# Attention weights turned by 32x32 blocks on the vector engine and 16 DMAs a group, in place of PE transposes

## The chip, the cores and the metric

The kernel runs on one core of a Trainium2 chip. The metric is the device time of one launch in microseconds (us). A core has five engines that run side by side, each through its own instructions in their order: PE (matrix products; its weight loads are shown as PEld), DVE (vectors), ACT (activations and copies), POOL (not used here beyond the first microsecond) and SP, whose queue only issues DMAs. A DMA can also be issued from ACT's queue. Engines wait for one another, and for DMAs to land, on semaphores.

## The reference

A chunked attention feeds a channel mix. All inputs are float32.

```python
# attention: 8 batches, 8 heads, 576 positions, head size 64; chunks of 64 positions
scores = scale * (q_c @ k_c.T)                    # 64 x 64 in each chunk
attn = exp(scores - max) / (sum + 1e-9)
x = (attn @ v_c)  ->  (batch, position, 512)
# channel mix
x_prev = x shifted by one position inside its batch
xk = mu_k * x + (1 - mu_k) * x_prev
xr = mu_r * x + (1 - mu_r) * x_prev
k = relu(xk @ w_k)                                # 512 -> 1024
out = sigmoid(xr @ w_r) * ((k * k) @ w_v)         # 512 -> 512, 1024 -> 512
```

## The kernel before

The 4608 positions are worked through in 18 groups of 256, each of two tiles of 128 positions (two chunks each). The matrix products of the channel mix run in three passes, since each operand is split into a high and a low part (`hi`, `lo`): `pk` is `xk @ w_k`, `pr` is `xr @ w_r`, `pv` is `k*k @ w_v`.

Steps are recorded by `do(fn, engine)` under a task's name and played back in an order written out by hand: `START` for the opening (groups 0 and 1, and the loading and splitting of weights), and then `GROUP`, once for each of the groups 2 to 17. Nothing reorders them afterwards; an engine's queue is what `GROUP` says. In `GROUP`, a word is a task, with a dot and the numbers of its steps (all, where there are none). For group g:

- `K0` to `K3` are four quarters of the k-branch of group g itself: product on PE, then relu, square, `hi` on ACT and `lo` on DVE. `R0`, `R1`: product and sigmoid. `V0`, `V1`: steps 0 to 7 are eighths of the product, step 8 multiplies by the sigmoid on DVE (L672) and issues the DMA of `out` from SP. The letter's digit is the tile.
- `Sa`, `Sb` are the scores and the softmax of the next group's tiles a and b (2g+2, 2g+3): step 0 product `s`, 1 row maximum, 2 subtraction, 3 exp on ACT, 4 sums, 5 division. `Pa`, `Pb` are their values: step 0 turns the weights on PE into `pt`, 1 copies them to `pT` on ACT, 2 is the product `xps` with `v`, 3 and 4 bring it to `x` in SBUF (the copy of L131 on ACT).
- `Mka`, `Mkb`, `Mra`, `Mrb` mix x with its predecessor on DVE (`d` L510, `mixk` and `mixr` L540, `lo` L559, with `hi` on ACT between), which gives `xk` and `xr` of the next group.
- `Tc`, `Td` turn q and k of the tiles 2g+4 and 2g+5 in 32x32 blocks on DVE (L339), which the next group's `Sa` and `Sb` read. `Lq`, `Lk`, `Lv` issue the loads of q and k for group g+3 and of v for group g+2 from SP.

Loads of q and k come as 16 DMAs each, because a DMA here moves one band of 32 partitions of one head pair. A group of 256 positions that crosses the end of a batch of 576 takes 32 DMAs each: `segments` cuts it. That is so for the groups 6, 11, 13 and 15, whose loads are issued in the groups 3, 8, 10 and 12. They are called cut groups below; in the groups 15 and 16 nothing is left to load of q and k.

Attention weights have 128 rows (positions) and 512 columns (8 heads by 64 keys). For `xps` they must have the keys on the partitions. Before, four transposes through PE with an identity matrix do this for a tile, and one copy on ACT takes them from PSUM.

PSUM pools bound how far products run ahead: `ps_k` has two buffers for `pk`, `ps_o` two for `pr` and `pv`, `ps_s` one for `s` and `pt`. `relu`, `out` and the loads' tiles have two buffers.

Of the kernel before, what the change touches and what calls it, by code (L numbers as in the profile page):

```python
# [7 lines left out]
F32 = mybir.dt.float32  # L8
# [8 lines left out]
P = 128  # L17
CH = 64
TT = 128
G = 256  # L20
# [32 lines left out]


GROUP = """
Lq K0.0 Sa.0 Sb.0 Sa.12 K0.123 Sa.3 Sb.12 K0.4 Sb.3 Sa.45 Sb.45 K1 K2.0 Pa.0 K2.1234 Pa.1
K3.0 Pb.0 Pb.1 K3.1234 Tc R0 Pa.2 Pb.2 Pa.34 Pb.34 Lv Lk Mka R1 Mkb Mra Mrb Td V0 V1
"""


# [18 lines left out]
def tile_chunk_attention_channel_mix(  # L79
# [12 lines left out]
    nc = tc.nc  # L92
    B, H, S, D = q.shape
    DM, FF = w_k.shape
    w_k, w_v, w_r = (w.bitcast(I32) for w in (w_k, w_v, w_r))
    HP = H // 2
# [2 lines left out]
    NCH = S // CH  # L99
    NG = B * S // G  # L100
    out_f = out.rearrange("b s c -> (b s) c")
    engine = dict(A=nc.scalar, D=nc.vector, G=nc.gpsimd)

    const = ctx.enter_context(tc.tile_pool(name="const", bufs=1))
    wts = ctx.enter_context(tc.tile_pool(name="wts", bufs=1))
# [1 line left out]
    tmp = ctx.enter_context(tc.tile_pool(name="tmp", bufs=2))  # L107
# [9 lines left out]
    do = Steps()  # L117
    T = {}
# [10 lines left out]
    def copy(e, to, x):  # L129
        if e == "A":  # L130
            nc.scalar.activation(to, x, AF.Copy)  # L131
        elif e == "D":
            nc.vector.tensor_copy(out=to, in_=x)  # L133
        else:
            nc.gpsimd.tensor_scalar(to, x, 1.0, 0.0, ALU.mult, ALU.add)
# [38 lines left out]
    def load_v(t):  # L174
        do.task = f"v{t}"

        def fn(_):
            vt = T[f"v{t}"] = att.tile([P, HP, 2, D], F32, tag="v", name=f"v_{t}", bufs=2)
            for e in range(2):
                b, c = divmod(2 * t + e, NCH)  # L180
                for j in range(2):
                    nc.sync.dma_start(  # L182
                        out=vt[j * CH : (j + 1) * CH, :, e, :],
                        in_=v[b, j * HP : (j + 1) * HP, c * CH : (c + 1) * CH, :].rearrange(
                            "h t d -> t h d"
                        ),
                    )

        do(fn, "Q")

    def load_blocks(g):
        for nm, src in (("q", q), ("k", k)):
            do.task = f"b{nm}{g}"

            def fn(_, nm=nm, src=src):
                dst = T[f"{nm}{g}"] = ld.tile([P, HP, G // 32, 32], F32, tag=nm, name=f"{nm}_{g}")
                for s, n in segments(g * G, G):
                    b, t0 = divmod(g * G + s, S)
                    for j in range(2):
                        for dh in range(2):  # L200
                            pp = j * 64 + dh * 32
                            for hp in range(HP):
                                nc.sync.dma_start(
                                    out=dst[pp : pp + 32, hp, s // 32 : (s + n) // 32, :],
                                    in_=src[
                                        b, j * HP + hp, t0 : t0 + n, dh * 32 : (dh + 1) * 32
                                    ].rearrange("(t i) d -> i t d", i=32),
                                )

            do(fn, "Q")  # L210
# [16 lines left out]
    def wv_tile(s, h):  # L227
        if (s, h) not in wv:
            wv[s, h] = wts.tile([P, NF // 2, DM], F32R, tag=f"wv{s}_{h}", name=f"wv{s}_{h}")
        return wv[s, h]  # L230
# [76 lines left out]
    halves = [slice(j * CH, (j + 1) * CH) for j in range(2)]  # L307
# [22 lines left out]
    def att_qk(t):  # L330

        g, tl = divmod(t, 2)
        tb = slice(tl * (TT // 32), (tl + 1) * (TT // 32))
        part = slice(tl * TT, (tl + 1) * TT)
        do.task = f"T{t}"
        for nm, to in (("q", qT), ("k", kT)):

            def f_move(_, nm=nm, to=to):
                nc.vector.transpose(  # L339
                    out=to[:, :, part].rearrange("p h (t i) -> p h t i", i=32),  # L340
                    in_=T[f"{nm}{g}"][:, :, tb, :],
                )

            do(f_move, "D")
# [59 lines left out]
    def x_cuts(t):  # L404

        cut = -t * TT % S
        if 0 < cut < TT:
            return [(0, cut, 0), (cut, TT - cut, cut + 1)]
        return [(0, TT, 0)]

    def att_values(t):
        do.task = f"P{t}"

        g, tl = divmod(t, 2)

        def f_tr(_):
            if tl == 0:
                T[f"pt{g}"] = ps_s.tile([P, 2, HP, TT], F32, tag="s", name=f"pt_{g}")
            for hp in range(HP):
                nc.tensor.transpose(  # L420
                    out=T[f"pt{g}"][:, tl, hp, :],
                    in_=T[f"p{t}"][:, 2 * hp : 2 * hp + 2, :],
                    identity=ident,
                )

        def f_pT(e):
            pT = T[f"pT{t}"] = att.tile([P, HP, TT], F32, tag="pT", name=f"pT_{t}")
            copy(e, pT, T[f"pt{g}"][:, tl])

        def f_pv(_):  # L430
            if tl == 0:
                T[f"xps{g}"] = ps_x.tile([P, NB, G], F32, tag="x", name=f"xps_{g}")
            for a in range(HP // 2):
                for e in range(2):
                    for c in range(2):
                        for j in range(2):
                            hp = 2 * a + c
                            nc.tensor.matmul(  # L438
                                T[f"xps{g}"][
                                    halves[c], 2 * j + a, tl * TT + e * CH : tl * TT + (e + 1) * CH  # L440
                                ],
                                T[f"v{t}"][halves[j], hp, e, :],
                                T[f"pT{t}"][halves[j], hp, halves[e]],
                                start=True,
                                stop=True,
                            )

        def f_open(_):

            x = xt[t] = xp.tile([P, NB, TT + 2], F32, tag="x", name=f"x_{t}")  # L450
            for s, n, c in x_cuts(t):
                if (t * TT + s) % S == 0:
                    nc.vector.memset(x[:, :, c : c + 1], 0.0)
                else:
                    seg = x_cuts(t - 1)[-1]
                    last = seg[2] + seg[1]
                    nc.vector.tensor_copy(
                        out=x[:, :, c : c + 1], in_=xt[t - 1][:, :, last : last + 1]
                    )

        def f_x(e):
            xps = T[f"xps{g}"][:, :, tl * TT : (tl + 1) * TT]
            for s, n, c in x_cuts(t):
                copy(e, xt[t][:, :, c + 1 : c + 1 + n], xps[:, :, s : s + n])

        do(f_tr, "P")
        do(f_pT, "A")
        do(f_pv, "P")
        do(f_open, "D")
        do(f_x, "A")  # L470
# [217 lines left out]
    for i in range(4):  # L688
        h = i // 2
# [5 lines left out]
            lambda s, h=h, part=part: wv_tile(s, h)[:, part, :],  # L695
            ("kk0", "kk1", "st", "st")[i],
        )
    for t in range(6):
        move_qk(t)
        att_scores(t)  # L700
        att_values(t)
        x_mix(t)
        if t in (1, 3):
            g = t // 2
            for fp in range(NF // 2):
                moe_k(g, fp)
            for tl in range(2):
                moe_r(g, tl)
# [9 lines left out]
    with tc.manual_schedule():  # L718
        for word in START.split():
            name, _, e = word.partition(":")  # L720
# [9 lines left out]
    def group(g):  # L730
        if g + 3 < NG:
            load_blocks(g + 3)
        if g + 2 < NG:
            for t in (2 * g + 4, 2 * g + 5):
                load_v(t)
                att_qk(t)
        if g + 1 < NG:
            for t in (2 * g + 2, 2 * g + 3):
                att_scores(t)
                att_values(t)  # L740
                x_mix(t)
        for fp in range(NF // 2):
            moe_k(g, fp)
        for tl in range(2):
            moe_r(g, tl)
            moe_v(g, (tl,))
        steps = do.take()
        tile_of = dict(zip("abcd", range(2 * g + 2, 2 * g + 6)))
        for word in GROUP.split():
            task, _, numbers = word.partition(".")  # L750
            if task == "Lv":
                names = [f"v{2 * g + 4}", f"v{2 * g + 5}"]
            elif task[0] == "L":
                names = [f"b{task[1]}{g + 3}"]
            elif task[-1] in tile_of:
                names = [f"{task[:-1]}{tile_of[task[-1]]}"]
            else:
                names = [f"{task[0]}{g}{task[1:]}"]
            for name in names:
                for i in numbers or range(NF + 1):  # L760
                    if f"{name}.{i}" in steps:
                        fn, e = steps.pop(f"{name}.{i}")
                        fn(e)
        assert not steps
# [30 lines left out]
```

## Time and profile before

| | |
|---|---|
| median of 3 runs | 617.06 us (616.78 to 619.68) |
| the profiled execution | 620.49 us, its span 618.7 us |
| mean granted TensorE clock | 0.988 |
| PE busy | 601.6 us (97%) |
| DVE, ACT busy | 399.8 us (65%), 332.5 us (54%) |
| chain that ended last, share of PE | 91% |
| transposes `pt` on PE | 144 instructions, 22.0 us busy |
| copies `pT` on ACT | 36 instructions, 21.3 us busy |

Times within the span are counted from the first instruction. Products on PE are pipelined and their rows overlap, so they are best read by their starts, or by the chain of waits, which gives each piece the time that it alone takes. SPq is the queue of SP: a row's time is that of issuing the DMAs, not that of moving the data.

### The profile page before, as it was taken

The numbers are of one execution on the slowest core, as the hardware profiler recorded it, in microseconds if no ns is written. First come the engines' busy times: TensorE is split into PE (matmuls) and PEld (weight loads), VectorE is DVE, ScalarE is ACT, GpSimd is POOL, SyncE is SP. The second block draws the span as 40 slices with busy tenths as digits, with TensorE's granted clock in tenths as the row PEclk, the third lists the DMA queues.
The fourth block names the chain that finished last, engine by engine and source line by source line (L and its number), as shares of the span: only waits on it lengthen the run. The fifth ranks groups of instructions, "written<-read, shape, count | busy, mean of one in ns | idle before, by whom it ended". The sixth has DMA issues, their size and how long they took to land.

```text
span 618.7 us, 14035 instructions
## 1 busy us (share of the span) xinstructions
PE 601.6 (97%) x5676; PEld 529.2 (86%) x5676; DVE 399.8 (65%) x860; ACT 332.5 (54%) x519; POOL 0.7 (0%) x6
## 2 busy tenths in 40 slices
PE   5888999999999999999999999999999999999997
PEld 5778988989898989888888888898989898989895
DVE  2767879757666667666666666666766667675610
ACT  4767684454545464646463737372728282827250
POOL 0000000000000000000000000000000000000000
PEclk9798999999999999999999999999999999999999
DMA  8796343244233434242322442234233334020000
GB/s 190 219 280 172 105 109 78 43 88 94 36 56 75 105 70 85 52 90 48 75 52 39 90 98 34 56 79 103 34 62 68 74 77 83 19 57 13 18 18 34
DMA packets 195071, 49.17 MB, mean 79 GB/s; under 512 B 186816, under 2 KB 186816, under 8 KB 195008
## 3 DMA queue, kind: packets, MB, share of 16 engines
q1 hardware_dynamic: 193952, 48.29, 34.9%
q8 instruction: 44, 0.72, 0.5%
q10 hardware_dynamic: 1056, 0.00, 0.1%
q14 instruction: 19, 0.16, 0.1%
HBM read 38.80 MB, written 9.44 MB: 78 GB/s over the span
## 4 chain that ended last, share of the span: by engine, by line
PE 91%; DMA 4%; SPq 3%; DVE 1%; issue 0%; ACT 0%; DVEq 0%
PE pk L580 33%; PE pv L659 33%; PE pr L629 16%; PE xps L438 3%; PE s L363 3%; DMA wk_st<-in_moe_w_k 3%; PE pt L420 2%; SPq L165 2%; SPq L182 1%; DMA wr_st<-in_moe_w_r 1%; PE mxk L528 1%; PE mxr L528 0%; SPq L254 0%; DVE wk_st L265 0%; DVE wk L280 0%
## 5 line engine op out<-in xcount | busy, mean ns | idle before, releaser
L580 PE MATMUL pk<-xkhi,wk 128*128 128x256 f32 x1152 | 217.9, 285 | 1.9 <-DVE wk L133 1.1
L659 PE MATMUL pv<-wv,kk 128*128 128x512 f32 x864 | 205.4, 395 | 0.0
L659 PEld LDWEIGHTS pv<-wv,kk 128*128 128x128 f32 x864 | 161.4, 187 | 39.2 <-DVE wv L280 0.2
L580 PEld LDWEIGHTS pk<-xkhi,wk 128*128 128x128 f32 x1152 | 181.3, 189 | 4.2 <-DVE wk L133 1.3
L580 PE MATMUL pk<-xklo,wk 128*128 128x256 f32 x576 | 162.3, 282 | 0.0
L580 PEld LDWEIGHTS pk<-xklo,wk 128*128 128x128 f32 x576 | 109.3, 190 | 0.9
L594 ACT ACTIVATE relu<-pk 128x512 f32<-128x512 f32 x72 | 42.6, 592 | 99.3 <-PE pk L580 99.3
L613 DVE TENSOR_TENSOR kk<-relu,kk 128x512 fp32r<-128x512 f32 x72 | 49.5, 687 | 69.9 <-ACT kk L131 69.9
L629 PE MATMUL pr<-wr,xrhi 128*128 128x512 f32 x288 | 93.7, 406 | 0.0
L629 PEld LDWEIGHTS pr<-wr,xrhi 128*128 128x128 f32 x288 | 51.4, 188 | 11.0
L629 PE MATMUL pr<-wr,xrlo 128*128 128x512 f32 x144 | 56.8, 395 | 0.0
L373 DVE TENSOR_REDUCE m<-s 128x8 f32<-128x512 f32 x36 | 24.7, 687 | 47.8 <-PE s L363 47.8
L131 ACT ACTIVATE xkhi<-mixk 128x512 fp32r<-128x512 f32 x32 | 20.2, 632 | 58.2 <-DVE mixk L540 58.2
L131 ACT ACTIVATE xrhi<-mixr 128x512 fp32r<-128x512 f32 x31 | 19.6, 632 | 57.0 <-DVE mixr L540 57.0
L131 ACT ACTIVATE kk<-relu 128x512 fp32r<-128x512 f32 x72 | 45.6, 633 | 2.1
L601 ACT ACTIVATE relu<-relu 128x512 f32<-128x512 f32 x72 | 45.5, 632 | 2.1
L540 DVE SCALAR_TENSOR_TENSOR mixk<-d,muk,x 128x128 f32<-128x128 f32 (+1 forms) x144 | 38.5, 332 | 1.0
L540 DVE SCALAR_TENSOR_TENSOR mixr<-d,mur,x 128x128 f32<-128x128 f32 (+1 forms) x144 | 38.3, 331 | 0.0
L559 DVE TENSOR_TENSOR xrlo<-mixr,xrhi 128x512 fp32r<-128x512 f32 x32 | 22.2, 692 | 21.0 <-ACT xrhi L131 21.0
L559 DVE TENSOR_TENSOR xklo<-mixk,xkhi 128x512 fp32r<-128x512 f32 x32 | 22.1, 692 | 20.9 <-ACT xkhi L131 20.9
L672 DVE TENSOR_TENSOR out<-pv,sg 128x512 f32<-128x512 f32 x36 | 24.0, 675 | 16.7 <-PE pv L659 15.7
L131 ACT ACTIVATE pT<-pt 128x512 f32<-128x512 f32 x36 | 21.3, 591 | 22.6 <-PE pt L420 22.6
(75 smaller groups left out, 562.9 us busy)
## 6 DMA issues: line engine op xcount, KB each, us to landing
v<-in_v SPq DMA_DIRECT2D x144, 64.0 KB, 2.5
out<-out SPq DMA_DIRECT2D x36, 256.0 KB, 2.2
q<-in_q SPq DMA_DIRECT2D x160, 32.0 KB, 2.0
k<-in_k SPq DMA_DIRECT2D x160, 32.0 KB, 2.0
wk_st<-in_moe_w_k SPq DMA_DIRECT2D x4, 1024.0 KB, 8.1
wv_st<-in_moe_w_v SPq DMA_DIRECT2D x4, 1024.0 KB, 7.2
wr_st<-in_moe_w_r SPq DMA_DIRECT2D x2, 1024.0 KB, 8.1
qn<-in_q SPq DMA_DIRECT2D x10, 128.0 KB, 2.9
```

The source lines that it names most:

```text
L131: nc.scalar.activation(to, x, AF.Copy)
L363: nc.tensor.matmul(scores()[halves[e], j, hp, :], qT[halves[j], hp, cols[e]], kT[halves[j], hp, cols[e]], start=True, stop=True,)
L373: nc.vector.tensor_reduce(out=heads(m), in_=scores(), axis=AX.X, op=ALU.max)
L540: nc.vector.scalar_tensor_tensor(out=m[:, cb, s : s + w], in0=d[:, cb, s : s + w], scalar=mu[:, cb : cb + 1], in1=x[:, cb, c : c + w], op0 ...
L559: engine[e].tensor_tensor(lo[:, :, part], T[f"m{nm}{t}"], hi[:, :, part].bitcast(F32), ALU.subtract)
L580: nc.tensor.matmul(pk[:, e, :], wk[a][:, cb, f * P : (f + 1) * P], xk[b][:, cb, :], start=(n == 0), stop=(n == 3 * NB - 1),)
L594: nc.scalar.activation(r, T[f"pk{g}{fp}"], AF.Relu)
L601: nc.scalar.activation(r, r, AF.Square)
L613: engine[e].tensor_tensor(lo, T[f"r{g}{fp}"], hi.bitcast(F32), ALU.subtract)
L629: nc.tensor.matmul(pr, xr[a][:, cb, tl * TT : (tl + 1) * TT], wr[b][:, cb, :], start=(n == 0), stop=(n == 3 * NB - 1),)
L659: nc.tensor.matmul(T[f"pv{g}{tl}"], kk[a][:, f, tl * TT : (tl + 1) * TT], wv[b, f // 4][:, f % 4, :], start=(f == 0 and n == 0), stop=(f = ...
L672: nc.vector.tensor_tensor(o, T[f"pv{g}{tl}"], T[f"sg{g}{tl}"], ALU.mult)
```

## The change

From group 2 on (the opening keeps PE's way), tiles a and b are turned in three moves:

1. `f_blocks`, in place of `f_tr`: one instruction of DVE for a tile turns each 32x32 block of the weights where it stands and writes it into `turned`, a tile of two halves in one buffer. 30 of these replace 120 transposes of PE.
2. `f_swap`, in place of `f_pT`: 16 DMAs for a group, each of 32 rows of 1 KB, carry block k of band w to band k, block w of the other half of `turned`, for both tiles at once. 12 of them (w 0 to 2) are issued from SP as step 1 of `Pa`, 4 (w 3) from ACT as step 1 of `Pb`. 30 copies of ACT fall away.
3. `xps` reads its 64 columns of weights as two runs of 32.

`GROUP` is written anew: the block turns stand behind `Sa.45` and `Sb.45`, the DMAs behind `Pb.0`, the loads `Lk Lv` ahead of `R1`, and the product `xps` comes after `R1` and five eighths of `V0`, where it stood between `R0` and `R1`. `Mka` to `Td` stay behind it and now follow `R1`. Lines of the changed program are 25 higher from L438 on.

```diff
 GROUP = """
-K3.0 Pb.0 Pb.1 K3.1234 Tc R0 Pa.2 Pb.2 Pa.34 Pb.34 Lv Lk Mka R1 Mkb Mra Mrb Td V0 V1
+R0 K3.1234 Tc Lk Lv R1 V0.01234 Pa.2 Pb.2 Pa.34 Pb.34 Mka Mkb Mra Mrb Td V0.5678 V1
...
+        def f_blocks(_):
+            if not turned:
+                turned["x"] = tmp.tile([P, 2, 4, 2, HP, 32], F32, tag="st", name="turned", bufs=1)
+            nc.vector.transpose(
+                out=turned["x"][:, 0, :, tl, :, :],
+                in_=T[f"p{t}"].rearrange("p (h j) (k c) -> p (j k) h c", j=2, k=2),
+            )
+
+        def f_swap(e):
+            for w in ((0, 1, 2), (3,))[tl]:
+                for k in range(4):
+                    engine[e].dma_start(
+                        out=turned["x"][32 * k : 32 * (k + 1), 1, w],
+                        in_=turned["x"][32 * w : 32 * (w + 1), 0, k],
+                    )
+
+        def weights(j, hp, e):
+            if blocks:
+                return turned["x"][halves[j], 1, 2 * e : 2 * e + 2, tl, hp, :]
+            return T[f"pT{t}"][halves[j], hp, halves[e]]
...
-                                T[f"pT{t}"][halves[j], hp, halves[e]],
+                                weights(j, hp, e),
...
-        do(f_tr, "P")
-        do(f_pT, "A")
+        do(f_blocks if blocks else f_tr, "D" if blocks else "P")
+        do(f_swap if blocks else f_pT, "QA"[tl] if blocks else "A")
...
-                att_values(t)
+                att_values(t, True)
```

The queue of SP in a cut group (8), before: loads of q, then v, then k, then the two stores. Of a name like `q_3782`, the number is the buffer's.

```order
L203 DMA q_3782<-in_q 32x2x32 x16
L203 DMA q_3782<-in_q 32x6x32 x16
L182 DMA v_4059<-in_v 64x4x64 x4
L182 DMA v_4064<-in_v 64x4x64 x4
L203 DMA k_4069<-in_k 32x2x32 x16
L203 DMA k_4069<-in_k 32x6x32 x16
L674 DMA out<-out_0_4180 128x512
L674 DMA out<-out_1_4208 128x512
```

The same stretch of SP's queue after, with the 12 DMAs of `turned`:

```order
L203 DMA q_3813<-in_q 32x2x32 x16
L203 DMA q_3813<-in_q 32x6x32 x16
L445 DMA turned<-turned 32x256 x12
L203 DMA k_4056<-in_k 32x2x32 x16
L203 DMA k_4056<-in_k 32x6x32 x16
L182 DMA v_4089<-in_v 64x4x64 x4
L182 DMA v_4094<-in_v 64x4x64 x4
L699 DMA out<-out_0_4216 128x512
L699 DMA out<-out_1_4244 128x512
```

The 12 DMAs stand behind all loads of q, and these behind the two stores of the group before; k now comes ahead of v.

PE around `xps` in group 9, before (between the products `pr` of the two tiles):

```order
L629 MATMUL pr_0_4418<-wr_103,xrhi_4142 128x512
L629 MATMUL pr_0_4418<-wr_104,xrhi_4142 128x512
L629 MATMUL pr_0_4418<-wr_103,xrlo_4143 128x512
L438 MATMUL xps_4433<-pT_4378,v_4059 64x64 x16
L438 MATMUL xps_4433<-pT_4409,v_4064 64x64 x16
L629 MATMUL pr_1_4510<-wr_103,xrhi_4142 128x512
```

And in group 8 after:

```order
L684 MATMUL pv_0_4114<-wv_1_953,kk_8_3911 128x512
L684 MATMUL pv_0_4114<-wv_1_959,kk_8_3911 128x512
L684 MATMUL pv_0_4114<-wv_1_953,kk_8_3912 128x512
L463 MATMUL xps_4130<-turned,v_3655 64x64 x16
L463 MATMUL xps_4130<-turned,v_3660 64x64 x16
L684 MATMUL pv_0_4114<-wv_1_953,kk_8_3911 128x512
```

`xps` has moved behind `R1` and within the product of `V0`, with 11 of the 16 eighths of `pv` (two tiles of eight) left in the group behind it.

DVE after the softmax of a tile in group 7, after; before, the rows of `turned` are not there and `p` is followed by the next row at once:

```order
L389 RECIPROCAL z_3503<-z_3503 128x8
L393 TENSOR_TENSOR p_3488<-p_3488,z_3503 128x512
L437 STREAM_TRANSPOSE turned<-p_3488 128x4x128
L387 TENSOR_REDUCE z_3509<-p_3499 128x8
L388 TENSOR_SCALAR z_3509<-z_3509 128x8
L389 RECIPROCAL z_3509<-z_3509 128x8
L393 TENSOR_TENSOR p_3499<-p_3499,z_3509 128x512
L437 STREAM_TRANSPOSE turned<-p_3499 128x4x128
L638 TENSOR_TENSOR kk_7_3494<-relu_1_3552,kk_7_3493 128x512
```

What moved here is only the two turns; `Mka` to `Td` and the two products of `out` keep their order on DVE behind `xps`.

More of the change, by code (lines that the diff above doesn't have):

```diff
@@ L55 @@
 GROUP = """
-Lq K0.0 Sa.0 Sb.0 Sa.12 K0.123 Sa.3 Sb.12 K0.4 Sb.3 Sa.45 Sb.45 K1 K2.0 Pa.0 K2.1234 Pa.1
-K3.0 Pb.0 Pb.1 K3.1234 Tc R0 Pa.2 Pb.2 Pa.34 Pb.34 Lv Lk Mka R1 Mkb Mra Mrb Td V0 V1
+Lq K0.0 Sa.0 Sb.0 Sa.12 K0.123 Sa.3 Sb.12 K0.4 Sb.3 Sa.45 Pa.0 Sb.45 Pb.0 Pa.1 K1 K2 Pb.1 K3.0
+R0 K3.1234 Tc Lk Lv R1 V0.01234 Pa.2 Pb.2 Pa.34 Pb.34 Mka Mkb Mra Mrb Td V0.5678 V1
 """
@@ L101, in tile_chunk_attention_channel_mix @@
     out_f = out.rearrange("b s c -> (b s) c")
-    engine = dict(A=nc.scalar, D=nc.vector, G=nc.gpsimd)
+    engine = dict(A=nc.scalar, D=nc.vector, G=nc.gpsimd, Q=nc.sync)
     const = ctx.enter_context(tc.tile_pool(name="const", bufs=1))
@@ L409, in x_cuts, with att_values @@
         return [(0, TT, 0)]
-    def att_values(t):
+    turned = {}
+    def att_values(t, blocks=False):
         do.task = f"P{t}"
```

## The prediction

> **What bounds the kernel now.** I read the page first, then the chain of waits in order of time, then the timelines of DVE, ACT and SP in one group. The page's line of busy time and its chain by engine say that PE is the bound:
>
> ```profile
> PE 601.6 (97%) x5676; PEld 529.2 (86%) x5676; DVE 399.8 (65%) x860; ACT 332.5 (54%) x519; POOL 0.7 (0%) x6
> PE 91%; DMA 4%; SPq 3%; DVE 1%; issue 0%; ACT 0%; DVEq 0%
> ```
>
> The chain (start, duration, piece) shows one whole group, with the first and the last start of a group that the change touches:
>
> ```profile
> 112.33 2.84 PE pk L580 x24
> ...
> 302.05 2.84 PE pk L580 x24
> 304.89 1.09 PE s L363 x64
> 305.98 5.88 PE pk L580 x48
> 311.86 0.44 PE pt L420 x4
> 312.30 2.85 PE pk L580 x24
> 315.14 0.44 PE pt L420 x4
> 315.58 2.80 PE pr L629 x12
> 318.38 1.09 PE xps L438 x64
> 319.47 3.00 PE pr L629 x12
> 322.47 11.20 PE pv L659 x48
> 333.67 2.84 PE pk L580 x24
> ...
> 586.63 11.36 PE pk L580 x96
> ```
>
> The 15 groups 2 to 16 lie between 112.33 and 586.63: 31.62 us each, all of it PE without a gap. So the question is whether PE stays fed. Softmax at the front of a group, and the work of ACT and DVE behind `xps` (start, duration; in brackets idle time before):
>
> ```profile
> 306.05 0.69 DVE L373 TENSOR_REDUCE m<-s 128x8 f32<-128x512 f32 x1 [3.27 <-PE s L363]
> ...
> 312.23 0.69 DVE L393 TENSOR_TENSOR p<-p,z 128x512 f32<-128x512 f32 x1
> ...
> 319.83 1.08 ACT L131 ACTIVATE x<-xps 128x512 f32<-128x512 f32 x2
> ...
> 332.39 0.67 DVE L339 STREAM_TRANSPOSE kT<-k 128x512 f32<-128x512 f32 x1
> 332.98 1.42 DVE L672 TENSOR_TENSOR out<-pv,sg 128x512 f32<-128x512 f32 x2
> ```
>
> From the copy of `x` (319.83) through the mixing to the end of `Td` (332.39 + 0.67 = 333.06) DVE takes 13.23 us, to the end of the second `out` (334.40) 14.57. `Td` ends before the group at 333.67 begins, and DVE idles some 3.3 us until the scores (as at 306.05). That is the slack of now.
>
> SP's queue, from a cut group (8) through group 9 to the next cut one:
>
> ```profile
> 303.22 16.33 SPq L203 DMA_DIRECT2D q<-in_q  x32
> 319.65 5.90 SPq L182 DMA_DIRECT2D v<-in_v  x8
> 325.59 16.52 SPq L203 DMA_DIRECT2D k<-in_k  x32
> 342.21 0.86 SPq L674 DMA_DIRECT2D out<-out  x2
> 343.12 9.25 SPq L203 DMA_DIRECT2D q<-in_q  x16
> 352.47 5.53 SPq L182 DMA_DIRECT2D v<-in_v  x8
> 358.05 8.43 SPq L203 DMA_DIRECT2D k<-in_k  x16
> 366.58 0.88 SPq L674 DMA_DIRECT2D out<-out  x2
> 367.51 15.96 SPq L203 DMA_DIRECT2D q<-in_q  x32
> ```
>
> It issues without a pause: the cut group takes 39.9 us of the queue (303.22 to 343.12), more than its 31.6 of PE, the other 24.4. Nobody waits for it now, since q and k are loaded a group or two ahead. The change puts something that PE needs in the same group behind these loads.
>
> **The change, part by part.** Times T are counted from the start of a group's `K0`.
>
> *The transposes leave PE.* Two pieces of 0.44 us a group: 31.62 - 0.88 = 30.74; over 15 groups 13.2 us. The copies `pT` leave ACT, which had room (54%): nothing.
>
> *`xps` moves back.* By the pieces, it now starts after K0 2.84, s 1.09, K1 and K2 5.88, K3 2.84, R0 2.80, R1 2.80 and 5/16 of 11.20 (3.50): T + 21.75, and ends at 22.84. Behind it stand 7.9 us of `pv` (11/16 of 11.20, and the 0.2 by which 3.00 exceeds 2.80 after `xps` now). DVE's work behind it is not shortened: `x` starts 0.07 after `xps` (as `m` at 306.05 after `s`), so `Td` ends at 22.84 + 0.07 + 13.23 = T + 36.14, which is 5.40 us into the next group. `Sb.0` needs it and was due there at 2.84 + 0.55 = 3.39. PE waits 2.0 us: the period is 32.8 instead of 31.62, a loss where the transposes alone would have gained. `xklo`, which `K0` needs, comes in time (6.4 us before `Td` ends).
>
> *The block turns on DVE.* 30 of them, priced by the same instruction on q:
>
> ```profile
> L339 DVE STREAM_TRANSPOSE qT<-q 128x512 f32<-128x512 f32 x30 | 21.2, 705 | 0.0
> ```
>
> The row maximum now follows `Td` and both `out`: T + 6.74. From `m` to the end of the second division is 6.9 us (306.05 to 312.92); with two turns of 0.7 the second is done at T + 15.0. Behind it `lo` of K1 waits, which the third eighth of `V0` needs some 6 us later. Cost nothing; without that cover 1.4 us a group.
>
> *The 12 DMAs on SP.* No row shows a DMA of 32 rows of 1 KB. Its issue is bounded by `out` (two in 0.86, 0.43 each, also one run a partition) and by q (16 in 9.25, 0.58, also 32 partitions; 0.51 in cut groups). I take 0.47, nearer `out` for its plain rows: 5.6 us for 12, ends 5.2 and 7.0. It can't be under nothing, since the queue issues one after another. Landing as q's:
>
> ```profile
> q<-in_q SPq DMA_DIRECT2D x160, 32.0 KB, 2.0
> ```
>
> They stand behind the loads of q, and these behind the second `out`, which waits for `Td`. A loop for a group that is not cut: q 9.35 (343.12 to 352.47), swaps 5.6, landing 2.0, `xps` 1.09, 0.07, DVE to the second `out` 14.57, its issue 0.5: 33.2 us. That is just above PE's 32.8. The swaps' own wait for DVE (T + 15.0) is over by then, as q ends at about T + 16.6. Behind them k, v and the stores are later; v waits for `xps`, and the stores come when `Td` is done anyway, so this costs nothing here. `xps` reads its weights in two runs of 32 instead of one of 64: I cost that at nothing, by 1.09 for `s` and `xps` alike; doubled, it would be 1.1 us a group.
>
> In a cut group the queue itself is the pace: 39.9 + 5.6 = 45.5 us from one group's q to the next's (the loop through `out` would need 39.8, and SP comes to the stores only at 44.6). PE waits for `turned`; what was hidden by prefetch is no longer.
>
> *The first group.* The opening's loads of k make the queue late there:
>
> ```profile
> 127.60 6.96 SPq L203 DMA_DIRECT2D q<-in_q  x14
> 134.68 6.46 SPq L182 DMA_DIRECT2D v<-in_v  x8
> ...
> 151.46 16.05 SPq L203 DMA_DIRECT2D q<-in_q  x32
> ```
>
> q ends at 134.68; swaps, landing and the rest as above (23.8) put group 3's q at 158.5 instead of 151.46: 7.1 us.
>
> *The 4 DMAs on ACT.* One such issue took 0.49 us:
>
> ```profile
> 0.73 0.49 ACTq L216 DMA_DIRECT2D muk<-in_moe_mu_k  x1
> ```
>
> 2.0 us from T + 15.0, before the sigmoid of `R0`, which PE delivers at 17.5: hidden. Their landing semaphores are shared with SP's DMAs, so in cut groups ACT stands with SP, and with it the sigmoid that frees a buffer for `V0`; PE then waits there instead of at `xps`, for the same queue.
>
> *PE's clock.* Waits can lower it. Stretches of the opening (length, PE busy, granted clock):
>
> ```profile
> 50.64:54.05 3.41, 1.66 (x66) 1.00 0.88 210
> 54.05:57.46 3.41, 3.19 (x15) 0.50 0.29 47
> ...
> 9.67:13.09 3.42, 0.34 (x4) 1.00 0.83 174
> 13.09:23.33 10.24, 7.03 (x85) 0.50 0.78 205
> ```
>
> After a stretch with 1.66 us busy the next ran at half clock, after one with 0.34 the next 10.24 us. A wait of 2.0 to 2.4 us may do the same: up to 1.7 us of PE's work lost, of which the loop's slack takes 0.4. In 8 uncut groups, about every second time: 5 us; ends 0 and 14. The Trainium skill, "TensorE: Matmul & The Clock Gate", section "HAM oscillation — how this bites in real kernels", allows idle gaps up to about 3.4 us; by it this term is 0 and the sum 695. The row of half clock after 1.66 us of work speaks against so wide an allowance, so I keep the 5.
>
> *The sum.* First group 7.1; four cut groups 4 x (45.5 - 31.6) = 55.6; eight others with loads 8 x (33.2 - 31.6) = 12.6; groups 15 and 16, without loads of q, 2 x 1.2 = 2.4; clock 5. Together 82.7. The profiled execution took 620.49 (span 618.7), which gives 703; it stands 3.4 above the median of the runs, 617.06, so I predict 617.06 + 82.7 = 700.
>
> **Rivals.** *B: issuing is cheap or hidden.* If the swaps cost SP next to nothing, or the queue runs far enough ahead, only PE's wait for `Td` is left: 15 x 1.2 = 18, so 635. Against it: every row of SP's queue is issued one after another, at 0.43 us or more. The Trainium skill, "DMA: Bandwidth & Descriptors", section "Issuing engines are not separate DMA queues", calls the sequencer's time to initiate a DMA "usually small relative to the DMA itself", which would lead here. The trace differs: 0.43 to 0.58 us of issue against 2.0 to land, and a queue full for 39.9 us.
>
> *C: faster, as the transposes alone say.* 617.06 - 13.2 = 604. It needs `Td` no later than 3.4 us into the next group, that is 11.2 us from `x` to `Td` instead of the 13.23 measured, and `turned` landed by T + 21.75. The 0.88 us a group do speak for it; nothing in DVE's rows speaks for a shorter way.
>
> *D: the clock falls for long.* If each long wait for SP is followed by 10.24 us at half clock, as at 13.09, about 5 us of PE's work are lost; in some 6 to 11 groups that is 30 to 55 us, partly hidden behind SP: 730. Against it: such groups wait for SP anyway.
>
> **Chances.** My case (A, the queue sets the pace in cut groups and `Td` the others) 0.78, B 0.11, D 0.06, C 0.03, no difference 0.02. A's own range is 688 to 720: with swaps at 5.2, uncut groups at PE's 32.8 and no clock term it is 700 - 2 - 3 - 5 = 690; with swaps at 7.0 in 13 groups 700 + 18 = 718. With a part of D above, and below the cases between A and B where part of the issue is hidden, 650 to 725. Slower by over 0.5% (3 us, about what a measurement of this kernel tells from no change): A, B and D, 0.95; faster 0.03; within 0.02.
>
> **What would show it.** In the profile after: PE's busy share near 85%; `s` waiting on DVE L339 by some 2 us in most groups; in the groups 3, 8, 10 and 12 PE waiting 5 us or more for ACT's sigmoid or a DMA of `turned`; SP's queue without a pause through them, its row `turned` x12 at 5 to 7 us; DVE idle for PE at L373 gone. I am wrong if the row of `turned` is far under 5 us, if `Td` ends before the next `K0`, or if PE's rows in cut groups have no wait.

## The result, and the profile after

The changed kernel takes 726.12 us (median of 3 runs, 723.55 to 726.32) against 617.06: 1.1738 times the time before, 95% interval 1.1706 to 1.1769. The forecast was 700, within 650 to 725; the change is slower, as forecast, by 26 us more than the forecast said, and 1 us above the upper end of its range. The profiled execution is the one of 726.12, its span 724.3.

The page's busy line, the granted clock in 40 slices, and the chain by engine:

```profile
PE 627.3 (87%) x5556; PEld 543.8 (75%) x5556; DVE 417.1 (58%) x890; ACT 317.5 (44%) x489; POOL 0.7 (0%) x6
PEclk8899999899798999999979898899989899999999
PE 32%; SPq 31%; DVE 15%; DMA 10%; ACT 6%; issue 5%; ACTq 0%; DVEq 0%
```

PE was 91% of the chain and is 32% now; SP's queue went from 3% to 31%. PE has 120 instructions fewer, yet is busy for 26 us longer: the mean granted clock fell from 0.988 to 0.929.

Two cut groups, 8 and 10, each followed by an uncut one, from `K0` to `K0` (stretch, its length, busy time and instructions of PE, PEld, DVE, ACT and POOL, granted clock, share of DMA, GB/s):

```profile
338.20:382.00 43.80, 34.77 (x297) 29.63 (x296) 22.89 (x52) 16.28 (x25) 0.00 (x0) 0.88 0.24 53
382.00:420.10 38.10, 33.57 (x297) 28.68 (x296) 20.95 (x47) 15.12 (x23) 0.00 (x0) 0.91 0.38 78
420.10:464.00 43.90, 34.94 (x298) 29.62 (x297) 23.51 (x61) 15.79 (x26) 0.00 (x0) 0.88 0.26 56
464.00:503.10 39.10, 32.65 (x298) 27.98 (x296) 21.43 (x47) 15.67 (x24) 0.00 (x0) 0.96 0.35 73
```

A group took 31.62 before. The 15 groups 2 to 16 now lie between the starts of `K0` at 109.3 and 692.1, 582.8 us against 474.3, so the whole loss of 109 is in them. SP's queue from group 8's loads of q through group 9:

```profile
345.39 16.45 SPq L203 DMA_DIRECT2D q<-in_q  x32
361.94 7.54 SPq L445 DMA_DIRECT2D turned<-turned  x12
369.53 16.50 SPq L203 DMA_DIRECT2D k<-in_k  x32
386.13 5.94 SPq L182 DMA_DIRECT2D v<-in_v  x8
392.17 1.02 SPq L699 DMA_DIRECT2D out<-out  x2
393.24 8.01 SPq L203 DMA_DIRECT2D q<-in_q  x16
401.35 7.55 SPq L445 DMA_DIRECT2D turned<-turned  x12
408.95 8.81 SPq L203 DMA_DIRECT2D k<-in_k  x16
417.87 5.34 SPq L182 DMA_DIRECT2D v<-in_v  x8
```

From q to q the cut group's round takes 47.85 us (345.39 to 393.24) without a pause. The 12 swaps take 7.5 to 7.6 of it, 0.63 each; their landing is quick, as the page's row of DMA issues says (1.9 us from issue to landing):

```profile
turned<-turned SPq DMA_DIRECT2D x180, 32.0 KB, 1.9
```

What was waited for (total us, times, longest):

```profile
ACT L668 <- DMA turned<-turned: 76.7, 14, 10.8
...
PE xps L463 <- DMA turned<-turned: 32.7, 21, 4.7
...
PE pv L684 <- ACT sg L668: 25.0, 6, 6.2
PE s L363 <- DVE kT L339: 23.7, 13, 3.0
```

These are PE's three new waits, 81 us together: for the swaps themselves, for a sigmoid that stands behind ACT's 4 swaps, and for `Td`. Line 668 is that sigmoid, with the loading of its table ahead of it.

### The profile page after: what moved, and what is told of

The parts are those of the page before. It is cut to its first block, busy times and chain, and to the rows that moved or that the text cites. A ratio compares the mean times of both kernels' runs of the same rounds, so it can differ in the third digit from the quotient of the medians.

```text
span 724.3 us, 14125 instructions
## 1 busy us (share of the span) xinstructions
PE 627.3 (87%) x5556; PEld 543.8 (75%) x5556; DVE 417.1 (58%) x890; ACT 317.5 (44%) x489; POOL 0.7 (0%) x6
## 3 DMA queue, kind: packets, MB, share of 16 engines
q1 hardware_dynamic: 202592, 54.20, 32.8%
## 4 chain that ended last, share of the span: by engine, by line
PE 32%; SPq 31%; DVE 15%; DMA 10%; ACT 6%; issue 5%; ACTq 0%; DVEq 0%
SPq L203 16%; PE pv L684 12%; PE pk L605 12%; SPq L445 9%; PE pr L654 4%; SPq L182 4%; DMA v<-in_v 3%; DMA wk_st<-in_moe_w_k 3%; PE xps L463 2%; DVE mixr L565 2%; DVE mixk L565 2%; DMA turned<-turned 2%; DMA q<-in_q 2%; DVE qT L339 1%; ACT xrhi L131 1%
## 5 line engine op out<-in xcount | busy, mean ns | idle before, releaser
L684 PE MATMUL pv<-wv,kk 128*128 128x512 f32 x864 | 226.5, 420 | 25.0 <-ACT sg L668 25.0
L684 PEld LDWEIGHTS pv<-wv,kk 128*128 128x128 f32 x864 | 172.1, 202 | 70.5 <-ACT sg L668 28.4
L605 PEld LDWEIGHTS pk<-xkhi,wk 128*128 128x128 f32 x1152 | 185.5, 195 | 4.3 <-DVE wk L133 1.3
L605 PEld LDWEIGHTS pk<-xklo,wk 128*128 128x128 f32 x576 | 112.5, 195 | 0.8
L131 ACT ACTIVATE x<-xps 128x512 f32<-128x512 f32 (+1 forms) x40 | 20.1, 554 | 100.8 <-PE xps L463 100.7
L463 PE MATMUL xps<-turned,v 64*64 64x64 f32 x960 | 27.1, 251 | 32.7 <-DMA turned<-turned 32.7
L463 PEld LDWEIGHTS xps<-turned,v 64*64 64x64 f32 x960 | 22.7, 159 | 40.6 <-DMA turned<-turned 25.2
L363 PE MATMUL s<-kT,qT 64*64 64x64 f32 x1152 | 26.4, 234 | 29.6 <-DVE kT L339 23.7
L363 PEld LDWEIGHTS s<-kT,qT 64*64 64x64 f32 x1152 | 21.5, 143 | 34.3 <-DVE kT L339 25.7
L131 ACT ACTIVATE kk<-relu 128x512 fp32r<-128x512 f32 x72 | 45.5, 632 | 2.1
L626 ACT ACTIVATE relu<-relu 128x512 f32<-128x512 f32 x72 | 45.5, 631 | 2.1
L482 DVE COPY x<-x 128x4 f32<-128x4 f32 x32 | 4.9, 154 | 68.2 <-ACT x L131 68.2
```

The costliest lines, as they stand in the source:

```text
L363: nc.tensor.matmul(scores()[halves[e], j, hp, :], qT[halves[j], hp, cols[e]], kT[halves[j], hp, cols[e]], start=True, stop=True,)
L463: nc.tensor.matmul(T[f"xps{g}"][halves[c], 2 * j + a, tl * TT + e * CH : tl * TT + (e + 1) * CH], T[f"v{t}"][halves[j], hp, e, :], weights ...
L605: nc.tensor.matmul(pk[:, e, :], wk[a][:, cb, f * P : (f + 1) * P], xk[b][:, cb, :], start=(n == 0), stop=(n == 3 * NB - 1),)
L626: nc.scalar.activation(r, r, AF.Square)
L684: nc.tensor.matmul(T[f"pv{g}{tl}"], kk[a][:, f, tl * TT : (tl + 1) * TT], wv[b, f // 4][:, f % 4, :], start=(f == 0 and n == 0), stop=(f = ...
```

## The experiments

Theory A is the prediction's: SP's queue sets the pace in the cut groups and the late `Td` in the others. Rivals were B (issuing is cheap or hidden, only `Td` counts) and D (the clock is a large part). All ratios are against the kernel before on the same chip, with their 95% intervals; the changed kernel stands at 1.1738. A hundredth is 6.2 us. The last column is from the profiled execution of each.

| | what is changed | ratio | interval | mean of groups 2 to 16, us |
|---|---|---|---|---|
| e1 | q loads behind the swaps | 1.1410 | 1.1354 to 1.1466 | 37.5 |
| e2 | `Td` next to `Tc` | 1.1420 | 1.1363 to 1.1477 | 37.4 |
| e3 | 8 swaps on SP, 8 on ACT | 1.1753 | 1.1707 to 1.1800 | 38.9 |
| e4 | k loads on POOL | 1.1343 | 1.1292 to 1.1394 | 37.0 |
| e5 | the kernel before in the new order, no swaps | 1.0685 | 1.0651 to 1.0718 | 34.3 |
| e6 | e1 and e4 together | 1.0636 | 1.0566 to 1.0707 | 34.7 |
| e7 | e6, PE's wait filled | 1.0476 | 1.0435 to 1.0516 | 33.5 |
| e8 | e1, e2, loads and 6 swaps on POOL | 1.0076 | 1.0029 to 1.0123 | 31.9 |
| e9 | as e8, no swap on ACT, 8 on SP, 8 on POOL | 0.9931 | 0.9907 to 0.9956 | 31.5 |
| e10 | as e9, 7 on SP, 9 on POOL | 0.9858 | 0.9826 to 0.9889 | 31.1 |
| e11 | the changed kernel, PE's wait at `s` filled | 1.1629 | 1.1593 to 1.1665 | 38.3 |
| e12 | e1, e2 and e4 together | 1.0220 | 1.0175 to 1.0265 | 32.3 |

**e1.**

```diff
-Lq K0.0 Sa.0 Sb.0 ... Pb.0 Pa.1 K1 K2 Pb.1
+K0.0 Sa.0 Sb.0 ... Pb.0 Pa.1 Lq K1 K2 Pb.1
```

> Edit: the loads of q move behind the 12 DMAs of turned in SP's queue; nothing else. Theory A (SP's queue is the pace, by its total of issues): the cut groups 3, 8, 10, 12 fall from 43.8 to 33-35 us, but each group after them rises from 38-40 to 46-48, since the backlog comes one group later; only group 2's late start (some 8 us) is saved. Time 705 to 718. Rival P (only the place of the swaps behind q's loads hurts, not the queue's total): cut groups fall to 34-35 and the others stay, 675 to 690. Rival B (PE's wait for Td is what costs): no change, 726.

Measured 704.88 us, at the lower edge of what A wrote. SP's queue in a cut group and the beginning of the next:

```profile
342.30 7.55 SPq L445 DMA_DIRECT2D turned<-turned  x12
349.90 16.38 SPq L203 DMA_DIRECT2D q<-in_q  x32
366.32 16.76 SPq L203 DMA_DIRECT2D k<-in_k  x32
...
389.72 7.56 SPq L445 DMA_DIRECT2D turned<-turned  x12
```

The swaps of the cut group are in time now, and the next group's start 47.4 us later, behind 33 us of loads. Groups after cut ones took 48.5 to 50.9, more than A's 46 to 48; the others took 30.9 to 35.5. The order in the queue moves the loss; the length of the queue stays.

**e2.**

```diff
-R0 K3.1234 Tc Lk ... Mka Mkb Mra Mrb Td V0.5678 V1
+R0 K3.1234 Tc Td Lk ... Mka Mkb Mra Mrb V0.5678 V1
```

> Edit: Td moves from the end of the mixing to Tc, ahead of xps; nothing else. Theory A: the waits of the scores (24 us in all) vanish, but the loop q, swaps, xps, mixing, out keeps its other terms, so an uncut group gains only the 1.3 us of the two turns and a cut one next to nothing: 700 to 712. Rival B: the groups return to PE's 30.7 us, 620 to 640.

Measured 704.55 us, as A wrote. No wait of `s` for `kT` on DVE is left, so the 23.7 us at `s` were `Td`'s. The two other waits stay and grow:

```profile
PE xps L463 <- DMA turned<-turned: 34.9, 25, 5.3
...
PE pv L684 <- ACT sg L668: 30.1, 13, 6.0
```

The gain did not stay in the uncut groups, as A had it: the four pairs of a cut group and the one behind it fell by 10 us together, from 331 to 321.

**e3.**

```diff
-            for w in ((0, 1, 2), (3,))[tl]:
+            for w in ((0, 1), (2, 3))[tl]:
```

> Edit: 8 of the 16 DMAs of turned are issued from SP and 8 from ACT, instead of 12 and 4. Theory A: SP issues 4 x 0.63 = 2.5 us less in each of the 13 groups with loads, 695 if ACT's 4.2 us of issues are hidden, about 705 if they hold up the sigmoid that V0 waits for. Rival B: no change, 726. Rival D (the time is PE's clock): no change to speak of.

Measured 726.37 us, no change: a miss for theory A, also in the milder form that ACT holds the sigmoid. The time is the one that B and D wrote; the waits show that something else cancelled. SP's share fell to 5.0 us and PE's wait at `xps` from 32.7 to 7.7, but ACT's 8 issues took 6.25 us and the sigmoid came behind them:

```profile
354.77 6.25 ACTq L445 DMA_DIRECT2D turned<-turned  x8
361.04 1.28 ACT L668 ACT_TABLE_LOAD   x1 [8.21 <-DMA turned<-turned]
362.34 0.60 ACT L668 ACTIVATE sg<-pr 128x512 f32<-128x512 f32 x1
```

PE's wait for the sigmoid rose from 25.0 to 43.3 us. What was saved at `xps` is lost at `V0`. The issues themselves took 0.52 to 0.60 each. Before the second, third and fourth (at 355.75, 356.93 and 357.93) ACT waited until one of SP's loads of q had landed (at 355.73, 356.91 and 357.91), since the DMAs of both queues share their landing semaphores. So DMAs on an engine that feeds PE's path cost that engine their issue, and here other queues' landings too.

**e4.**

```diff
-                                nc.sync.dma_start(
+                                (nc.gpsimd if nm == "k" and g > 4 else nc.sync).dma_start(
```

> Edit: the loads of k for the groups from 5 on are issued from POOL's queue, which is idle, instead of SP; q, v, swaps and stores stay on SP. Theory A: SP loses 8 to 16 us of issues a group; the cut groups keep their own 42-44 us (q still stands ahead of the swaps), the groups after them fall from 38-40 to 34-35: about 700. Rival B: no change, 726. If POOL's issues are much slower than SP's, k comes late and Tc waits; the row of POOL's DMAs will say.

Measured 700.91 us, as theory A says. POOL's issues of k in one uncut group, 0.58 each:

```profile
197.05 9.22 POOL L203 DMA_DIRECT2D k<-in_k  x16 [24.74 <-DVE kT L339]
```

The groups behind cut ones fell from 38.1 to 40.7 us to 31.7 to 33.6; the cut groups stayed at 43.1 to 44.6, since q still stands ahead of the swaps.

**e5.** The kernel before with only its order changed:

```diff
-K3.0 Pb.0 Pb.1 K3.1234 Tc R0 Pa.2 Pb.2 Pa.34 Pb.34 Lv Lk Mka R1 Mkb Mra Mrb Td V0 V1
+K3.0 Pb.0 Pb.1 R0 K3.1234 Tc Lk Lv R1 V0.01234 Pa.2 Pb.2 Pa.34 Pb.34 Mka Mkb Mra Mrb Td V0.5678 V1
```

> The kernel before, with its transposes on PE and its copies on ACT kept, no block turn and no swap; only the order of a group is the changed kernel's (R0 ahead of K3.1234, the loads ahead of R1, the weighting of values behind five eighths of V0, Td behind it). Theory A (the later xps alone costs PE a wait for Td): by the pieces xps ends at about T + 23.7 (22.84 and the two transposes of 0.44), Td 13.3 later at 37.0, which is 5.4 into the next group, where it is due at 3.4; PE waits some 2.0 us a group at s, 15 x 2.0 = 30, so 647, and with 5 to 20 us of lower clock 650 to 667. Half clock over 30 us, waits at s for L339 in most groups, none for q. Rival (the order is harmless, and only the swaps cost): 612 to 622, no wait at s.

Measured 659.96 us: the new order alone costs 42 us, with no swap in the program, and the wait that it brings is for `Td` behind the later `xps`. The half clock is less than expected (19 us where over 30 was written). PE waits at `s` and nowhere else from group 2 on:

```profile
PE s L363 <- DVE kT L339: 30.6, 14, 3.0
```

**e6.** The edits of e1 and e4 together.

> The changed kernel with both reliefs of SP's queue at once: k loads on POOL, and q loads behind the swaps. SP then issues swaps, q and v, at most 7.6 + 16.4 + 5.5 + 1 = 30.5 us in a group. Theory A (queue ahead of the swaps and PE's wait for Td are the whole loss): the swaps no longer wait for the queue, and what is left is Td: 32.8 to 33.2 a group with 5 to 25 us of lower clock, 635 to 660; PE's gaps at xps and pv under 10 us together, those at s 25 to 35. Rival (the swaps' own length, 7.6 us of issue and 1.9 of landing behind the second block turn, makes xps late even in an empty queue): gaps at xps of 20 us or more, 665 to 690.

Measured 658.84 us, or 656 by the ratio; its profiled execution is the longest of its four (652.44 to 662.76, granted clock 0.971 to 0.948), so its rows may stand a little high. With the loads gone from ahead of the swaps, hardly a gap is left at `xps` (0.3 us) or `pv`, and 30.7 us at `s`:

```profile
PE s L363 <- DVE kT L339: 30.7, 14, 3.0
```

e1 and e4 gained 20 and 24 us alone and gain 68 together: either one leaves loads ahead of the swaps in one group of each pair, of the cut one and the one behind it. Most groups take 34.4, not the 32.8 that a wait of 2.0 gives, and the granted clock is 0.95 in the two shown:

```profile
314.50:348.90 34.40, 32.41 (x297) 28.48 (x296) 21.94 (x49) 15.86 (x24) 17.41 (x32) 0.95 0.27 66
348.90:383.40 34.50, 32.50 (x298) 28.44 (x297) 22.19 (x50) 15.87 (x24) 9.22 (x16) 0.95 0.40 89
```

**e7.** The kernel of e6 with products of zeros that only fill the wait:

```diff
         def f_s(_):
...
+            for _ in range(8 if tl and t > 5 else 0):
+                nc.tensor.matmul(
+                    scores()[:, 0, 0:2, :], idle,
+                    idle.rearrange("p (h c) -> p h c", h=2), start=True, stop=True)
```

> The kernel of e6 with 8 matmuls of zeros (128 x 128) ahead of the second tile's scores in each group from 2 on, written where those scores are then written anew: they stand where PE waits for Td and only fill that wait. Theory A with the clock (a wait of 2 to 3 us at s costs a stretch of half clock behind it, about half of which comes on the path): half clock in the trace falls to under a third of e6's, and the time falls by 5 to 20 us under e6. Rival (the clock is hidden, since the loop through Td sets the period and not PE's work): half clock falls as much, time within 3 us of e6.

Measured 646.17 us; by the ratios 0.016 or 10 us less than e6, intervals apart, and half clock behind the opening fell from 58.7 us to 2.9. Two groups to set beside those of e6:

```profile
342.70:375.80 33.10, 33.10 (x314) 29.03 (x313) 22.07 (x49) 15.65 (x24) 9.23 (x16) 1.00 0.41 91
375.80:408.80 33.00, 33.00 (x314) 28.91 (x312) 21.88 (x53) 15.71 (x25) 17.36 (x32) 1.00 0.31 74
```

More work on PE makes it faster: the waits of 2 to 3 us had cost 1.2 us a group through the clock (34.7 to 33.5 in the mean). What stays is the loop through `Td`, 32.9 to 33.3 in nine groups and up to 34.2 in the others.

**e8.** q behind the swaps, `Td` early, and on POOL three quarters of the loads of k and 6 swaps:

```diff
+                                (nc.gpsimd if nm == "k" and g > 4 and pp else nc.sync).dma_start(
...
+                    (nc.gpsimd if (w, k) in ((1,2),(1,3),(2,0),(2,1),(2,2),(2,3)) else engine[e]).dma_start(
```

> The changed kernel with Td next to Tc, q loads behind the swaps, three quarters of the k loads and 6 of SP's 12 swaps issued by POOL (6 stay on SP, 4 on ACT). Theory A (the loss was only the queue and Td, and PE's 0.88 us a group is real): no wait is left at s, the swaps take 3.8 us beside each other and end at about T + 20.7, before xps at T + 21.75, and the period is PE's 30.74: 604 to 615, faster than before by 0.5 to 2 per cent. Rival (POOL's issues interfere, or waits on shared landing semaphores spread the queue's delay): PE gaps over 20 us at xps or pv, 622 or more.

Measured 623.04 us, 8 us above A's 604 to 615 and above the time before: A's gain did not come, and the time is one that the rival wrote. The rival's gaps of over 20 us at `xps` or `pv` are not there. Undisturbed groups take 30.86, as the removed transposes promised; most of the rest is the sigmoid behind ACT's 4 issues, and in its part the rival was right: ahead of the second, third and fourth of those shown, ACT waited for the landing of two of SP's loads of v and of a store.

```profile
343.90 6.00 ACTq L445 DMA_DIRECT2D turned<-turned  x4
349.93 1.28 ACT L668 ACT_TABLE_LOAD   x1 [7.36 <-DMA turned<-turned]
```

```profile
PE pv L684 <- ACT sg L668: 8.5, 7, 3.4
```

**e9** and **e10.** The kernel of e8, with no swap on ACT:

```diff
+                    (nc.gpsimd if w > 1 else nc.sync).dma_start(            # e9
+                    (nc.gpsimd if 4 * w + k > 6 else nc.sync).dma_start(    # e10
```

> The kernel of e8 with no swap left on ACT: 8 of the 16 on SP, 8 on POOL. In e8 ACT waited 67.4 us in 15 groups at its 4 issues, the sigmoid stood behind them, and PE waited for it ahead of V0. Theory A (that wait is all that keeps e8 from the gain): no wait of pv for the sigmoid, 8 issues of 0.7 on SP and of 0.5 on POOL end by T + 19.5 and land by 21.5, just ahead of xps at T + 21.75; 30.86 a group, 604 to 612. Rival (the landing of the longer rows of 8 is now late): gaps of 1 to 2 us at xps in most groups and half clock behind them, 620 to 635.

> The same with 7 swaps on SP and 9 on POOL, since an issue took 0.71 us on SP and 0.50 on POOL in e8: both rows end within 0.5 us of each other, 0.5 us earlier than SP's 8. Theory A: 604 to 612, no more than 2 us from e9, and the better one where e9 shows gaps at xps. Rival (POOL is the slow one, as in e4, where 16 issues took 9.2 us, 0.57 each): 5.2 us on POOL, gaps at xps larger than in e9, 2 to 10 us slower than it.

e9 measured 614.57 us (0.9931), a little above what A wrote, and e10 610.42 (0.9858), within it, and 4 us below e9 where A allowed 2: both are faster than before by intervals that leave out 1, though by less than 2%. In e9's trace five gaps of 0.3 to 1.1 us are left at `xps`, in e10's two of 0.5 and 0.7. The rows of SP and POOL in one group of e10 are equally long:

```profile
342.04 4.38 SPq L445 DMA_DIRECT2D turned<-turned  x7
```

```profile
340.51 4.47 POOL L445 DMA_DIRECT2D turned<-turned  x9 [13.10 <-issue]
```

PE in e10 (the page's busy line, and two groups):

```profile
PE 590.0 (97%) x5556; PEld 516.6 (85%) x5556; DVE 416.5 (68%) x890; ACT 316.1 (52%) x489; POOL 181.7 (30%) x345
```

```profile
264.60:295.40 30.80, 30.80 (x298) 26.93 (x297) 22.00 (x50) 15.65 (x24) 11.34 (x21) 1.00 0.40 87
295.40:326.10 30.70, 30.70 (x298) 26.86 (x297) 21.87 (x49) 15.65 (x24) 16.16 (x31) 1.00 0.30 71
```

**e11.** The changed kernel with the filling of e7.

> The changed kernel with e7's 8 matmuls of zeros ahead of the second tile's scores, which fill PE's waits for Td at s and nothing else. Theory A (the queue sets the period, so the clock is mostly hidden behind it): half clock falls from 90.7 us to 40 to 60, since the waits at pv and xps stay; the time falls by no more than 8 us, 717 to 727. Rival D (the clock is a large part of the loss): it falls by 10 to 25 us, as from e6 to e7 (12.7 us), 700 to 716.

Measured 718.32 us; by the ratios 0.0109 or 7 us less, at the upper edge of what A allowed and under D's 10. Half clock fell from 90.7 us to 61.7, where A wrote 40 to 60. The mean clock rose from 0.929 to 0.949. That the waits at `pv` and `xps` lower the clock too is plain from the trace (a stretch of 10.24 us at half clock in each of the four cut groups); what these cost on the path was not tried.

**e12.** The edits of e1, e2 and e4, with all swaps where the change put them.

> The changed kernel with k loads on POOL, q loads behind the swaps and Td next to Tc, but all 12 swaps still on SP and 4 on ACT: the queue is free when the swaps are due and no score waits for Td. What is left is the swaps' own length. Theory A: they start at about T + 13.9 (as in e8), 7.6 us of issue and 1.9 of landing put them at T + 23.4 against xps due at T + 21.75, and the loop through xps and DVE runs at 31.8 to 32.5 a group; with ACT's 4 issues in front of the sigmoid as in e8, 618 to 634. Rival (the landing semaphores shared between the queues hold SP or ACT as in e3): gaps at pv and xps over 40 us together, 640 or more.

Measured 630.49 us, as A wrote. In an empty queue the swaps still take 8 us, and land after `xps` was due; ACT's 4 still hold the sigmoid:

```profile
348.83 7.83 SPq L445 DMA_DIRECT2D turned<-turned  x12
```

```profile
PE xps L463 <- DMA turned<-turned: 8.8, 12, 1.0
...
PE pv L684 <- ACT sg L668: 4.8, 7, 1.1
```

So with everything around them in place, the swaps still keep the kernel 14 us (0.022) above the time before. e10 divides them between two queues, neither of them ACT's (and leaves a quarter of the loads of k on SP), and is 9 us (0.0142) below it.

## Why the prediction was right in direction and short in size

*The transposes leave PE: right.* Forecast 30.74 us a group; e10 runs 30.73 in nine of the 15 groups and 31.0 to 32.1 in the others. The gain of 13 us is real and was hidden under the rest; e10 shows 9 of it. It also shows that `xps` in two runs of 32 costs nothing that counts, as forecast.

*`Td` is late by 2.0 us: right, and it was priced too low.* In e5 and e6 PE waits at `s` 14 times, 2.2 us on average. e7, where only that loop is left at full clock, runs at 33.5 in the mean where 32.8 was forecast. What the term left out, above all, is what the wait does to the clock.

*The issue of a swap: the step that failed.* I took 0.47 us, nearer `out` for its plain rows, with an upper end of 7.0 for 12. It was 0.63, 7.54 to 7.55 for 12, beyond that end. A dearer row had been shown and not used as an end: v, 8 in 5.53, 0.69 each. Where the queue is the pace, this is what the sum lacked. With 7.6 for the swaps, a cut group and the one behind it become 47.5 + 35.2 = 82.7 in place of 78.7; 8 and 9 took 81.9, 10 and 11 83.0, the first such pair 82.0 and the last 84.5. The four pairs are 16.6 us over the forecast, group 2 is 2.7 over.

*The other groups: a term too small, and luck.* 2.0 us more in each of the 13 groups with loads would be 26 us, just what is missing between 82.7 and the 109 measured, but the match is luck. The groups 5 to 7 and 14 took 34.5 to 35.6, which the 33.2 + 2.0 of the queue's loop would fit, but PE's waits in them are for `Td` at `s`, 2.0 to 3.0 in each, and only in group 7 also at `xps` (2.3). e6 takes 34.4 in such groups with no load ahead of the swaps. These four are 7.2 us over the forecast, and the groups 15 and 16, which have no loads of q, 4.4: 11.6 us by the wait for `Td` and the clock, where the sum had 5 for the clock. In e11, where the wait is filled, the four fall by 2 us together and the two by 3, and PE waits about 1 us at `xps` in 5, 6 and 7, so the queue's loop stands close behind `Td`'s.

*The cut groups alone at 45.5: the total of a pair right with 7.6 for the swaps, the place not.* The cut groups took 43.3 to 43.9 and those behind them 38.1 to 40.7, where 33.2 was forecast. Part of a cut group's delay shows only in the next, since the late loads of k and v stand ahead of its stores and q; with k on POOL (e4) the groups behind fall to 31.7 to 33.6.

*ACT's 4 DMAs hidden: wrong.* I priced them at 2.0 us beside other work, and named the sigmoid only for cut groups. Their rows take 2.45 us in the groups 15 and 16 of the changed kernel, where SP has no loads of q, and 2.84 to 4.59 in the others, where ACT also waits for landings of SP's loads of q; and from e8 to e9, where they go, the ratio falls by 0.0145, 9 us (SP and POOL issue two more each). e3 shows the same from the other side.

*The block turns at no cost: right where loads of q hold SP longer.* The 30 took 0.71 each, and DVE's idle time for PE at the row maximum, where they lie, fell from 47.8 us to 6.2. In e12 it is no longer so: in 12 of 15 groups SP issues the first swap within 0.04 us of the end of the second turn, so there the turns lie ahead of the swaps that `xps` waits for.

*The clock at 5: too low for the wait at `s`.* Filling it gains 7 us in e11 and 10 in e6. I let every second wait cost a stretch; in e6's profile each of the 14 does. The Trainium skill, "TensorE: Matmul & The Clock Gate", section "HAM oscillation — how this bites in real kernels", allows idle gaps up to about 3.4 us. The longest wait at `s` was 3.0, and the clock was 0.95 with it and 1.00 without; the measurement decides, and the rule is too wide for this kernel.

How many waits cost a stretch is a matter of where they fall. e5 has the same waits as e6 (30.6 us in 14), and only 4 of its 14 are followed by half clock. In the traces the clock changes on a grid of 3.41 us. Here are two waits of 2.0 us of e5, cut by this grid (stretch, its length, busy time and instructions of PE, granted clock). The first lies within one piece, and the next piece runs at half clock; the second lies over two, and the clock stays:

```profile
146.99:150.40 3.41, 1.43 (x44) 1.00 0.34 77
150.40:153.81 3.41, 3.41 (x19) 0.50 0.54 173
...
283.52:286.93 3.41, 2.75 (x50) 1.00 0.02 5
286.93:290.35 3.42, 2.10 (x44) 1.00 0.20 74
290.35:293.76 3.41, 3.41 (x31) 1.00 0.58 137
```

Of the 41 waits at `s` in the changed kernel, e5 and e6, all 24 that put 1.80 us or more into one piece were followed by half clock from the end of that piece, and none of the 17 that put 1.73 or less into each. No run shifted the waits against the grid to test this; it is read off these traces.

*The rivals.* B falls: the issue is neither cheap nor hidden. Even its case, a queue far enough ahead (e6), is 1.0636 or 656 us, not 635, by the clock and the longer waits. "DMA: Bandwidth & Descriptors", section "Issuing engines are not separate DMA queues", of the Trainium skill says that issuing on several engines saves only the sequencers' time, "usually small relative to the DMA itself". The trace agrees with the first half (landing, 1.9 us in the changed kernel, is 1.8 to 2.1 in e10) and not with the second: e12 and e10 differ by 22 us only in which queues issue the swaps and a quarter of k. C was right about the 0.88 us a group and about its own condition, which e10 meets with `Td` ahead of `xps` and with other queues. D's 730 is nearer to the 726 measured than my 700 is, and its mechanism is there: half clock in 17 stretches behind the opening, 10.24 us at a time in three of the four cut groups. But filling the waits at `s` takes away a third of the half clock (29 of 90.7 us) for 7 us, and it leaves three of the four pairs of a cut group and the one behind it within 1.1 us of what they took. How much of what is left at `pv` and `xps` lies on the path stays open.

## What to carry to other kernels

Count a queue's issues like instructions of an engine: so many DMAs at 0.4 to 0.7 us each, added up over the stretch in which they must be out, and see what they stand behind. Work that leaves the bound engine pays only if what replaces it is in time; here the same change is 17% slower or 1.4% faster by where 16 DMAs, some loads and two turns stand. Put DMAs that PE waits for ahead of prefetches, on queues whose engine has nothing on the path, and remember that a wait of 2 us on PE costs more than 2 us when the clock falls behind it.

## What was unexpected of the hardware

The time to issue a DMA depends on its kind and on the engine, not on the bytes alone. In the changed kernel SP's median was 0.366 us for a store of `out` (256 KB), 0.448 for a load of q (32 rows), 0.589 for a swap of 32 KB within SBUF and 0.615 for one of v. POOL issued the same swap in 0.496 (e10) where SP took 0.588, but a load of k in 0.584 (e4) where SP takes 0.448. ACT issues a swap in 0.520, yet four of them took 2.45 to 6.00 us in a row. Four issues with no wait between them take 2.45; in the longer rows ACT waits, between two issues, for the landing of a DMA of SP's (in e8's 6.00, until 349.37 for a store of `out` issued at 345.06).

A wait of 2 to 3 us once in 34 us of work was enough for a stretch of 3.41 or 6.83 us at half clock behind it in each of 14 groups of e6, and products of zeros in its place kept the clock at 1.00. In e5 the same waits cost it in 4 groups of 14, as they fall across the grid of 3.41 us.
